# Score matmuls of two attention units in turns, with their PSUM banks shared with the weighted sums

## The chip, the cores and the metric

The kernel runs on one core of a Trainium2 chip. The metric is device time in microseconds (us) of one execution; lower is better. Engines are named as in the profile: PE (TensorE matmul), PEld (its weight loads), DVE (VectorE), ACT (ScalarE), POOL (GpSimd), SP (SyncE, which issues most DMAs). Matmul results go to PSUM, which has 8 banks of 128 partitions; a tile here takes one bank.

## The reference

Three stages follow each other: attention, a dense SoLU layer with layer norm, and a layer of eight experts of which each token uses one. Only the first is touched.

```python
def _attn_ref(q, k, v):                       # 4 batches, 8 heads, 576 positions, 64 columns
    scores = scale * np.matmul(q, k.transpose(0, 1, 3, 2))
    mask_local   = (rel >= 0) & (rel < 32)                       # heads 0 to 3
    mask_strided = (rel >= 0) & (pos[None, :] % 32 == pos[:, None] % 32)   # heads 4 to 7
    scores = np.where(masks, scores, -1e9)
    attn = exp(scores - max); attn = attn / (sum(attn) + 1e-9)
    return np.matmul(attn, v)
...
h = x @ w_in; solu = h * softmax(h); ln = layernorm(solu) * g_ln; x = ln @ w_out
e = argmax(x @ w_gate + bias[modality]); out = gate * (relu(x @ w1[e]) @ w2[e])
```

## The kernel before

**Attention.** Heads are handled in pairs `hp` (two heads, j = 0 and 1); pairs 0 and 1 are local, 2 and 3 strided. `qT` and `kT` hold a pair transposed: head 0 in partitions 0-63, head 1 in partitions 64-127 for local pairs. For strided pairs the sequence is cut into 8 residues (`SG = 8`, 72 positions each), and residue t stands in partitions 0-63 if it is even and in 64-127 if it is odd. A score matmul contracts over 64 rows, so it reads only one half of the partitions. Each pair gives four units of work. A local unit is three tiles of 96 queries by 128 keys of one head; a strided unit is four tiles of 72 by 72 of one head, all of even or all of odd residues. All tiles of one unit thus lie in one half of the partitions.

**One unit.** `scores` (line 311) issues its score matmuls (line 326) into one PSUM bank called S, DVE adds the mask and takes the maximum (line 332), POOL or DVE subtracts it (338), ACT takes the exponential (341), DVE sums (356) and takes reciprocals (357, 358), POOL normalises (364). `probs_T` transposes the result on PE (372, tile pP) and ACT copies it to pT (374). When both units of a head pair's group are there, `weighted` (377) multiplies with V into one bank called po (383); head j's sums go to output partitions 64j to 64j+63. ACT copies po to xTH (395) and DVE writes the remainder to xTL (396). Score and weighted-sum matmuls are float32, and the trace has two records for each of them.

**The dense layer** runs beside attention on the same engines: ph (line 475, x @ w_in), pn (518, transposes), pa and pb (531, @ w_out). The start also converts float64 weights: DVE, ACT and POOL work of lines 203 to 261 (wf, winH, winL, woH, woL).

**Banks.** Eight banks: "h" 2 (ph, and S of the first batch), "T" 2 (transposes), "y" 2 (pa, pb), "S" 1 (S of batches 1 to 3), "o" 1 (po).

**Order.** The kernel emits work in slots (a unit's stages A, T, P, V, and the table `TAKES` that says how many slots stand between dense steps). A scheduler then simulates a timeline and sets each engine's final order, and with it, tile by tile, which bank of a tag a tile gets. Engines run that order in sequence, so an instruction that waits holds up all behind it on its engine.

Of the kernel before, what the change touches and what calls it, by code (L numbers as in the profile page):

```python
# [9 lines left out]
F32 = mybir.dt.float32  # L10
# [18 lines left out]
def tile_attention_moe_moe2(  # L29
# [15 lines left out]
    nc = tc.nc  # L45
    B, H, S, D = q.shape
    NT, DM = out.shape
    NE, _, FF = w1.shape
    P = 128
    STRIDE = 32  # L50
# [75 lines left out]
    def flip_tile(out_, in_, eye):  # L126
        return nc.tensor.transpose(out_, in_, eye)

    warm_out = ps.tile([P, 2 * P], F32, name="warm", tag="S", bufs=1)

    def warm(n):
        wide = ident.bitcast(mybir.dt.bfloat16)
# [175 lines left out]
            dv = dst.rearrange("c (i p) -> c i p", p=SP_)[:, n * u:n * u + n]  # L308
        nc.scalar.copy(dv, pt[:, 0:n, :np_])

    def scores(b, hp, tiles, j, qT, kT):
        local = hp < H // 4
        nt = len(tiles)
        nq, nk = (QT, P) if local else (SP_, SP_)
        if b == 0:
            sp_ = ps.tile([P, 4, P], F32, name="S", tag="h")
        else:
            sp_ = ps.tile([P, 4, P], F32, name="S", tag="S", bufs=1)
        for i, t in enumerate(tiles):
            if local:  # L320
                half, q0, k0 = j, t * QT, t * QT
            else:
                half, q0 = t % 2, (j * SG + t) // 2 * SP_
                k0 = STRIDE + q0
            rows = slice(half * D, half * D + D)
            nc.tensor.matmul(  # L326
                sp_[:nq, i, :nk], qT[rows, q0:q0 + nq], kT[rows, k0:k0 + nk], start=True, stop=True)
        ex = at.tile([P, 4, P], F32, name="ex", bufs=4)
        mx = st.tile([P, 4], F32, name="mx")
        for i, t in enumerate(tiles):  # L330
            mk = maskL[:nq, min(t, 1)] if local else maskS
            nc.vector.tensor_tensor_reduce(  # L332
                ex[:nq, i, :nk], sp_[:nq, i, :nk], mk, 1.0, NEG, ALU.add, ALU.max,
                mx[:nq, i:i + 1])
        xb = SHIFT_ON[2 * b + (not local)]
        if xb != "0":
            eng = nc.gpsimd if xb == "P" else nc.vector
            eng.tensor_tensor(  # L338
                ex[:nq, :nt, :nk], ex[:nq, :nt, :nk],
                mx[:nq, :nt].unsqueeze(2).to_broadcast([nq, nt, nk]), ALU.subtract)  # L340
            nc.scalar.activation(ex[:nq, :nt, :nk], ex[:nq, :nt, :nk], AF.Exp, scale=SCALE)
            return ex, nq, nk, None
        nb = st.tile([P, 4], F32, name="nb")
        nc.vector.tensor_scalar(nb[:nq, :nt], mx[:nq, :nt], -SCALE, None, ALU.mult)
        den = st.tile([P, 4], F32, name="den")
        for i in range(nt):
            nc.scalar.activation(
                ex[:nq, i, :nk], ex[:nq, i, :nk], AF.Exp,
                bias=nb[:nq, i:i + 1], scale=SCALE, accum_out=den[:nq, i:i + 1])
        return ex, nq, nk, den  # L350
# [17 lines left out]
    def probs_T(tiles, ex, nq, nk):  # L368
        nt = len(tiles)
        pt = ps.tile([P, 4, P], F32, name="pP", tag="T")  # L370
        for i in range(nt):
            flip_tile(pt[:nk, i, :nq], ex[:nq, i, :nk], ident[:nq, :nq])
        pT = at.tile([P, 4, P], F32, name="pT", bufs=3)
        nc.scalar.copy(pT[:nk, :nt, :nq], pt[:nk, :nt, :nq])  # L374
        return pT

    def weighted(b, hp, tiles, nq, nk, pTs, vn):
        local = hp < H // 4
        nt, t0 = len(tiles), tiles[0]
        po = ps.tile([P, 4, P], F32, name="po", tag="o", bufs=1)  # L380
        for i, t in enumerate(tiles):
            for j in range(2):
                nc.tensor.matmul(  # L383
                    po[j * D:(j + 1) * D, i, :nq], vn[:nk, j, t], pTs[j][:nk, i, :nq],
                    start=True, stop=True)
        base = (b % 2) * S
        src = po[:, :nt, :nq]
        if local:
            o0 = base + t0 * QT
            dH, dL = [x[:, hp, o0:o0 + nt * QT].rearrange("c (t q) -> c t q", t=nt) for x in (xTH, xTL)]  # L390
        else:
            dH, dL = [
                x[:, hp, base:base + S].rearrange("c (p i) -> c i p", i=SG)[:, t0::2]
                for x in (xTH, xTL)]
        nc.scalar.copy(dH, src)
        nc.vector.tensor_tensor(dL, src, dH.bitcast(F32), ALU.subtract)

    def attention_slots():
        order = [(b, hp) for b in range(B) for hp in PAIRS[b]]
        units = []  # L400
        for b, hp in order:
            for tiles in ((0, 1, 2), (3, 4, 5)) if hp < H // 4 else ((0, 2, 4, 6), (1, 3, 5, 7)):
                for j in range(2):
                    units.append((b, hp, tiles, j))
        nat, tr, live = {}, {}, {}

        def load(n):
            if n < len(order):
                nat[n] = load_pair(*order[n])

        def transpose(n, part):
            if n < len(order):
                if part == 0:
                    tr[n] = alloc_pair(order[n][1])
                transpose_part(order[n][1], part, *nat[n][0:2], *tr[n])

        load(0)
        load(1)
        for part in range(4):
            transpose(0, part)  # L420
            warm(WARM)
        pts = {}

        def stage_a(n):
            if n < len(units):
                b, hp, tiles, j = units[n]
                live[n] = scores(b, hp, tiles, j, *tr[n // 4])
                normalise(b, hp, len(tiles), *live[n])

        def stage_t(n):  # L430
            if n < len(units):
                m, part = divmod(n, 4)
                transpose(m + 1, part)
                if part == 3:
                    load(m + 2)

        def stage_p(n):
            z = n - LAG
            if 0 <= z < len(units):
                b, hp, tiles, j = units[z]  # L440
                ex, nq, nk, den = live.pop(z)
                pts[z] = (probs_T(tiles, ex, nq, nk), nq, nk)

        def stage_v(n):
            z = n - LAG
            if 0 <= z < len(units):
                b, hp, tiles, j = units[z]
                if j == 1:
                    first, nq, nk = pts.pop(z - 1)
                    weighted(b, hp, tiles, nq, nk, (first, pts.pop(z)[0]), nat[z // 4][2])  # L450

        stages = dict(A=stage_a, T=stage_t, P=stage_p, V=stage_v)
        for n in range(len(units) + LAG):
            for c in STAGES:
                stages[c](n)
                yield

    def moe_a(t, front, between):
        g0 = (t % (NTILE // 2)) * P
        ts_ = slice(g0, g0 + P)  # L460
        e = mp.tile([P, 2, 512], F32, name="e")
        so = mp.tile([P, 2, 512], F32, name="so")
        mx = st.tile([P, 2], F32, name="hmx")
        hs = []
        for hf in range(2):
            if done_att and t % 2:
                ph = ps.tile([P, 512], F32, name="ph", tag=("S", "o")[hf], bufs=1)
            else:
                ph = ps.tile([P, 512], F32, name="ph", tag="h")
            hs.append(ph)  # L470
            cs = slice(hf * 512, hf * 512 + 512)
            n = 0
            for c in range(KD):
                for a, w in ((xTH, winH), (xTH, winL), (xTL, winH)):
                    nc.tensor.matmul(ph, a[:, c, ts_], w[:, c, cs], start=n == 0, stop=n == 3 * KD - 1)  # L475
                    n += 1
                if c == 1:
                    between()
            nc.vector.reduce_max(mx[:, hf:hf + 1], ph, axis=AX.X)
            if hf == 0:  # L480
                front()
                between(1)
        nb = st.tile([P, 1], F32, name="hnb")
        nc.vector.tensor_scalar(nb, mx[:, 0:1], mx[:, 1:2], -1.0, ALU.max, ALU.mult)
        s2 = st.tile([P, 2], F32, name="s2")
        for hf in range(2):
            nc.scalar.activation(e[:, hf], hs[hf], AF.Exp, bias=nb, scale=1.0, accum_out=s2[:, hf:hf + 1])
        a2 = st.tile([P, 2], F32, name="a2")
        for hf in range(2):
            nc.vector.scalar_tensor_tensor(  # L490
                so[:, hf], e[:, hf], 1.0, hs[hf], ALU.mult, ALU.mult, accum_out=a2[:, hf:hf + 1])
        return so, e, s2, a2
# [407 lines left out]
    def chunk_few(w, idx, j, side=(), then=None, blk=0, tiny=False):  # L900
# [6 lines left out]
        steps = TINY_STEPS if tiny else FEW_STEPS  # L907

        def up(q):
            p = ps.tile([P, 256], F32, name="pq", tag=("h", "h", "S", "o")[q], bufs=(2, 2, 1, 1)[q])  # L910
            f_ = slice(q * 256, q * 256 + 256)
            for c in range(KD):
                fl = dict(stop=c == KD - 1, skip_group_check=True)
# [299 lines left out]
```

## Time and profile before

| | |
|---|---|
| median of 3 runs (lowest to highest) | 718.24 us (717.89 to 719.5) |
| span of the profiled execution | 714.5 us, first to last instruction |
| median less span | 3.7 us |
| PE busy | 652.2 us, 91% of the span |
| DVE busy | 381.2 us, 53% |
| ACT busy, POOL busy | 298.5 us, 204.1 us |

The profiled execution has no time of its own beside its span; the 3.7 us by which the median of the runs is above the span is what lies around it. Attention's score matmuls run from 6.7 to 339.6 us of the span, its weighted sums from 18.5 to 355.8 us. Busy shares are means over stages with different limits, so the rows below are taken from stretches. PE intervals overlap, since matmuls are pipelined: what a matmul costs is read from one start to the next, not from its own duration.

### The profile page before, as it was taken

Reading aid. Unit: us, or ns where it says so; the run is one execution under the profiler, and the core shown is the slowest. Engines: PE = TensorE matmul, PEld = TensorE weight load, DVE = VectorE, ACT = ScalarE, POOL = GpSimd, SP = SyncE. Lnnn points to the kernel's source line nnn. Section 1 sums busy time; section 2 is a strip of 40 time slices with the busy share of each in tenths; the row PEclk is TensorE's granted clock in tenths of the full one; section 3 lists DMA queues with packets and bytes.
Section 4 is the critical chain, followed back from the end, with each engine's and each line's share of the span. In section 5 each row is a group of like instructions: output and inputs, shape, how many; then the busy total and the mean of one; then the engine's idle time right before and its main releaser. Section 6 shows DMA issues by size and latency. Waiting matters only on the chain. (4 is left out here: it accounts for less than half of the span.)

```text
span 714.5 us, 12636 instructions
## 1 busy us (share of the span) xinstructions
PE 652.2 (91%) x4540; PEld 565.4 (79%) x4540; DVE 381.2 (53%) x1361; ACT 298.5 (42%) x689; POOL 204.1 (29%) x253
## 2 busy tenths in 40 slices
PE   7688999999999999999999999999999999992954
PEld 6466877888888888888888998998898888882843
DVE  4999897567766666556488642235111121112761
ACT  3545654445545556667356421224111211211631
POOL 5876553111433242212003322232022112202410
PEclk9999978999999999999999999999999999996987
DMA  8735411023221122100061201446011011101770
GB/s 221 184 129 159 111 71 34 18 66 85 71 59 41 49 54 70 33 19 16 30 212 55 90 31 47 145 170 210 27 60 60 16 45 60 57 19 41 235 240 7
DMA packets 54696, 59.77 MB, mean 84 GB/s; under 512 B 39296, under 2 KB 39296, under 8 KB 54594
## 3 DMA queue, kind: packets, MB, share of 16 engines
q1 hardware_dynamic: 47954, 43.04, 20.5%
q0 software_dynamic: 4048, 10.78, 4.7%
q10 hardware_dynamic: 2592, 4.72, 1.9%
q8 instruction: 48, 0.79, 0.5%
q14 instruction: 54, 0.44, 0.2%
HBM read 48.79 MB, written 10.26 MB: 83 GB/s over the span
## 5 line engine op out<-in xcount | busy, mean ns | idle before, releaser
L881 DVE SCALAR_TENSOR_TENSOR winL<-pf,winL 128x512 fp32r<-128x512 f32 x36 | 24.9, 692 | 136.2 <-ACT winL L880 136.1
L834 PE MATMUL py<-w2H,winL 128*128 128x512 f32 x288 | 92.5, 396 | 0.0
L874 PE MATMUL pf<-xTH,w1H 128*128 128x256 f32 x288 | 82.4, 287 | 0.0
L874 PE MATMUL pf<-xTL,w1H 128*128 128x256 f32 x288 | 81.6, 283 | 0.0
L874 PE MATMUL pf<-xTH,w1L 128*128 128x256 f32 x288 | 81.5, 283 | 0.0
L364 POOL TENSOR_TENSOR ex<-ex,rd 96x384 f32<-96x384 f32 (+1 forms) x56 | 48.2, 863 | 100.1 <-DVE rd L358 69.2
L326 PE MATMUL S<-kT,qT 64*72 64x72 f32 (+1 forms) x448 | 63.5, 289 | 4.7 <-DVE mx L332 3.2
L880 ACT ACTIVATE winL<-pf 128x512 fp32r<-128x512 f32 x36 | 21.6, 599 | 99.7 <-PE pf L874 99.7
L834 PEld LDWEIGHTS py<-w2H,winL 128*128 128x128 f32 x288 | 53.5, 188 | 10.9
L326 PEld LDWEIGHTS S<-kT,qT 64*72 64x72 f32 (+1 forms) x448 | 49.3, 176 | 15.8 <-DVE mx L332 4.1
L475 PE MATMUL ph<-winH,xTH 128*128 128x512 f32 x144 | 61.1, 424 | 0.6 <-DVE so L490 0.5
L338 POOL TENSOR_TENSOR ex<-ex,mx 72x288 f32<-72x288 f32 (+1 forms) x40 | 34.6, 864 | 89.3 <-DVE mx L332 59.2
L475 PE MATMUL ph<-winH,xTL 128*128 128x512 f32 x144 | 58.8, 414 | 0.0
L475 PE MATMUL ph<-winL,xTH 128*128 128x512 f32 x144 | 58.8, 408 | 0.0
L874 PEld LDWEIGHTS pf<-xTH,w1H 128*128 128x128 f32 x288 | 56.4, 196 | 0.3
L874 PEld LDWEIGHTS pf<-xTL,w1H 128*128 128x128 f32 x288 | 56.4, 196 | 0.3
L874 PEld LDWEIGHTS pf<-xTH,w1L 128*128 128x128 f32 x288 | 56.4, 196 | 0.0
L840 POOL DMA_INDIRECT out_dram<-yo,idx x14 | 14.0, 1001 | 134.0 <-ACT yo L839 125.5
L531 PE MATMUL pa<-woH,nL 128*128 128x264 f32 x144 | 42.7, 296 | 1.3 <-DVE nL L521 1.3
L383 PE MATMUL po<-pT,vn 72*64 72x72 f32 (+1 forms) x448 | 37.4, 266 | 7.0 <-ACT pT L374 6.4
L531 PE MATMUL pa<-woH,nH 128*128 128x264 f32 x144 | 43.0, 299 | 0.4 <-ACT nH L520 0.4
L531 PE MATMUL pb<-woH,nH 128*128 128x256 f32 x144 | 41.4, 287 | 0.0
(257 smaller groups left out, 1657.7 us busy)
## 6 DMA issues: line engine op xcount, KB each, us to landing
raw<-in_moe_w_dram SPq DMA_DIRECT2D x37, 512.0 KB
y_d<-yt ACTq DMA_DIRECT2D x18, 256.0 KB
raw<-in_moe_w_in_dram SPq DMA_DIRECT2D x8, 512.0 KB
raw<-in_moe_w_out_dram SPq DMA_DIRECT2D x8, 512.0 KB
vn<-in_v_dram SPq DMA_DIRECT2D x16, 160.0 KB
qn<-in_q_dram SPq DMA_DIRECT2D x8, 288.0 KB
kn<-in_k_dram SPq DMA_DIRECT2D x8, 288.0 KB
vn<-in_v_dram SPq DMA_DIRECT2D x8, 288.0 KB
```

Source lines behind the costliest of these rows:

```text
L326: nc.tensor.matmul(sp_[:nq, i, :nk], qT[rows, q0:q0 + nq], kT[rows, k0:k0 + nk], start=True, stop=True)
L338: eng.tensor_tensor(ex[:nq, :nt, :nk], ex[:nq, :nt, :nk], mx[:nq, :nt].unsqueeze(2).to_broadcast([nq, nt, nk]), ALU.subtract)
L364: nc.gpsimd.tensor_tensor(ex[:nq, :nt, :nk], ex[:nq, :nt, :nk], rd[:nq, :nt].unsqueeze(2).to_broadcast([nq, nt, nk]), ALU.mult)
L383: nc.tensor.matmul(po[j * D:(j + 1) * D, i, :nq], vn[:nk, j, t], pTs[j][:nk, i, :nq], start=True, stop=True)
L475: nc.tensor.matmul(ph, a[:, c, ts_], w[:, c, cs], start=n == 0, stop=n == 3 * KD - 1)
L531: nc.tensor.matmul(p, a[:, f], w[:, f, cols], start=n == 0, stop=n == 3 * KF - 1)
L834: nc.tensor.matmul(p, a[:, f, s], x, start=n == 0, stop=n == 3 * KF - 1)
L840: nc.gpsimd.indirect_dma_start(out=out[:, :], out_offset=indirect(idx[:, col, 2:3].bitcast(U32)), in_=o, in_offset=None, bounds_check=NT - ...
L874: mm = nc.tensor.matmul(p[:, u], a[:, c, fs], x[:, c], start=n == 0, stop=n == 3 * KD - 1)
L880: last[0] = (nc.scalar.activation(hH[:, f2s], p, AF.Relu), nc.vector.scalar_tensor_tensor(hL[:, f2s], p, 0.0, hH[:, f2s].bitcast(F32), ALU ...
L881: nc.vector.scalar_tensor_tensor(hL[:, f2s], p, 0.0, hH[:, f2s].bitcast(F32), ALU.max, ALU.subtract))
```

## The change

The two units of a group become a pair that is laid out together. `raw_scores` is new: it takes two S banks at once, one for each half of the partitions, and issues the score matmuls of the two units in turns, first unit, second unit, first unit and so on. `scores` now only does what follows. Strided units are regrouped, so that unit u of group g holds the even (u = 0) or odd (u = 1) residues of both heads: tiles 4g+u and 4g+2+u for j = 0 and 1, and a group's four residues are contiguous. Before, a group held all even or all odd residues, and its two units were the two heads. The tag "S" has now two banks, which S and po share; "o" is gone. The dense layer's and the experts' uses of "S" and "o" become "S" throughout. Every engine has the same instructions as before, in the same number.

```diff
-    def scores(b, hp, tiles, j, qT, kT):
+    def raw_scores(b, hp, pair, qT, kT):
+        local = hp < H // 4
+        nq, nk = (QT, P) if local else (SP_, SP_)
+        banks = []
+        for _ in range(2):
+            if b == 0:
+                banks.append(ps.tile([P, 4, P], F32, name="S", tag="h"))
+            else:
+                banks.append(ps.tile([P, 4, P], F32, name="S", tag="S"))
+        for i in range(len(pair[0])):
+            for half in range(2):
+                t, j = pair[half][i]
+                if local:
+                    q0, k0 = t * QT, t * QT
+                else:
+                    q0 = (j * SG + t) // 2 * SP_
+                    k0 = STRIDE + q0
+                rows = slice(half * D, half * D + D)
+                nc.tensor.matmul(
+                    banks[half][:nq, i, :nk], qT[rows, q0:q0 + nq], kT[rows, k0:k0 + nk],
+                    start=True, stop=True)
+        return banks
...
-            sp_ = ps.tile([P, 4, P], F32, name="S", tag="S", bufs=1)
...
-        po = ps.tile([P, 4, P], F32, name="po", tag="o", bufs=1)
+        po = ps.tile([P, 4, P], F32, name="po", tag="S")
         for i, t in enumerate(tiles):
             for j in range(2):
+                half, at_ = place[t, j]
                 nc.tensor.matmul(
-                    po[j * D:(j + 1) * D, i, :nq], vn[:nk, j, t], pTs[j][:nk, i, :nq],
+                    po[j * D:(j + 1) * D, i, :nq], vn[:nk, j, t], pTs[half][:nk, at_, :nq],
                     start=True, stop=True)
...
-            for tiles in ((0, 1, 2), (3, 4, 5)) if hp < H // 4 else ((0, 2, 4, 6), (1, 3, 5, 7)):
-                for j in range(2):
-                    units.append((b, hp, tiles, j))
+            for g in range(2):
+                if hp < H // 4:
+                    pair = [[(t, j) for t in range(3 * g, 3 * g + 3)] for j in range(2)]
+                else:
+                    pair = [[(t, j) for t in (4 * g + u, 4 * g + 2 + u) for j in range(2)] for u in range(2)]
+                units += [(b, hp, pair, 0), (b, hp, pair, 1)]
...
-                ph = ps.tile([P, 512], F32, name="ph", tag=("S", "o")[hf], bufs=1)
+                ph = ps.tile([P, 512], F32, name="ph", tag="S")
```

What the scheduler makes of it differs by batch. First the order on PE at the first units of batch 0, in the kernel before (a number tells one tile from another; x4 is four matmuls in a row):

```order
L326 MATMUL S_181<-kT_148,qT_147 72x72 x4
L127 MATMUL ptq_202<-ident_77,qn_141 128x72 x4
L326 MATMUL S_218<-kT_148,qT_147 72x72 x4
L127 MATMUL ptq_247<-ident_77,qn_141 128x72 x4
L326 MATMUL S_263<-kT_148,qT_147 72x72 x4
```

and the same place after the change:

```order
L329 MATMUL S_181<-kT_148,qT_147 72x72
L329 MATMUL S_182<-kT_148,qT_147 72x72
L127 MATMUL ptq_207<-ident_77,qn_141 128x72 x4
L329 MATMUL S_181<-kT_148,qT_147 72x72
L329 MATMUL S_182<-kT_148,qT_147 72x72
L329 MATMUL S_181<-kT_148,qT_147 72x72
L329 MATMUL S_182<-kT_148,qT_147 72x72
L329 MATMUL S_181<-kT_148,qT_147 72x72
L329 MATMUL S_182<-kT_148,qT_147 72x72
L127 MATMUL ptq_247<-ident_77,qn_141 128x72 x4
```

Here the matmuls of the two units do stand in turns. Then a group of batch 1, S_1700 and its partner, on PE before:

```order
L383 MATMUL po_1691<-pT_1575,vn_817 64x96
L326 MATMUL S_1700<-kT_1217,qT_1216 72x72 x4
L127 MATMUL pn_1677<-ident_77,so_1315 128x128 x4
L127 MATMUL pn_1684<-ident_77,so_1315 128x128 x4
L383 MATMUL po_1691<-pT_1641,vn_817 64x96
L383 MATMUL po_1691<-pT_1575,vn_817 64x96
L383 MATMUL po_1691<-pT_1641,vn_817 64x96
L383 MATMUL po_1691<-pT_1575,vn_817 64x96
L383 MATMUL po_1691<-pT_1641,vn_817 64x96
L326 MATMUL S_1735<-kT_1217,qT_1216 72x72 x4
```

and after, where S_1701 is the second unit of S_1700's pair:

```order
L396 MATMUL po_1691<-pT_1580,vn_817 64x96
L329 MATMUL S_1700<-kT_1221,qT_1220 72x72 x4
L127 MATMUL pn_1677<-ident_77,so_1315 128x128 x4
L127 MATMUL pn_1684<-ident_77,so_1315 128x128 x4
L396 MATMUL po_1691<-pT_1641,vn_817 64x96
L396 MATMUL po_1691<-pT_1580,vn_817 64x96
L396 MATMUL po_1691<-pT_1641,vn_817 64x96
L396 MATMUL po_1691<-pT_1580,vn_817 64x96
L396 MATMUL po_1691<-pT_1641,vn_817 64x96
L329 MATMUL S_1701<-kT_1221,qT_1220 72x72 x4
```

Nothing has moved here: the two units stand as far apart as two units did before, and in the built program S_1700 and S_1701 have the same bank, po_1691 the other. Last, a strided weighted sum of batch 3 on PE, before:

```order
L383 MATMUL po_4165<-pT_4096,vn_3591 64x72
L326 MATMUL S_4230<-kT_4007,qT_4006 72x72 x4
L475 MATMUL ph_4497<-winH_71,xTH_75 128x512
```

and after, from the score matmuls that had the same bank just before it:

```order
L329 MATMUL S_4064<-kT_3682,qT_3681 72x72 x4
L127 MATMUL pP_4158<-ident_77,ex_4025 72x72 x4
L396 MATMUL po_4165<-pT_4101,vn_3591 64x72 x2
L329 MATMUL S_4176<-kT_4012,qT_4011 72x72 x4
L127 MATMUL pP_4203<-ident_77,ex_4073 72x72 x4
```

Before, one po matmul stood alone and seven followed when the second unit's pT was there; now two stand together and six follow, and po_4165 takes the bank that S_4064 had.

## Rows read from the trace of the kernel before

**Rows 1.** The page: span, and busy time of each engine.

```profile
span 714.5 us, 12636 instructions
PE 652.2 (91%) x4540; PEld 565.4 (79%) x4540; DVE 381.2 (53%) x1361; ACT 298.5 (42%) x689; POOL 204.1 (29%) x253
```

**Rows 2.** Stretches: from:to, length, busy us of each engine, clock, DMA share, GB/s.

```profile
18.00:36.00 18.00, 11.26 (x86) 9.07 (x86) 17.96 (x60) 10.13 (x23) 15.36 (x19) 1.00 0.76 186
...
72.00:126.00 54.00, 51.46 (x313) 41.84 (x313) 46.15 (x156) 30.44 (x73) 23.16 (x28) 0.87 0.24 71
126.00:360.00 234.00, 233.33 (x1878) 199.26 (x1877) 145.27 (x729) 127.12 (x358) 56.04 (x82) 1.00 0.17 47
```

**Rows 3.** The longest wait of PE, 72 to 486 us: total, times, longest.

```profile
PE po L383 <- ACT pT L374: 1.5, 1, 1.5
```

**Rows 4.** Score and weighted-sum matmuls by line, behind 126 us: ns min/median/max.

```profile
L326 PE MATMUL S<-kT,qT x288: 225/225/348, 132.3 to 339.6; 64*72 64x72 f32 x96, 64*96 64x128 f32 x48
...
L383 PE MATMUL po<-pT,vn x312: 226/236/297, 135.9 to 355.8; 72*64 72x72 f32 x96, 128*64 128x96 f32 x60
```

**Rows 5.** Score matmuls in flight (x) in stretches of 0.12 us.

```profile
20.44:20.56 0.12, 0.12 (x4) 1.00 1.04 16
...
20.92:21.04 0.12, 0.12 (x7) 1.00 1.33 19
```

**Rows 6.** Timeline of PE: start us, busy us, line, operation, count.

```profile
156.31 0.34 PE L383 MATMUL po<-pT,vn 72*64 72x72 f32 x2
156.58 0.39 PE L531 MATMUL pb<-woH,nH 128*128 128x256 f32 x1
...
159.09 0.28 PE L531 MATMUL pb<-woH,nH 128*128 128x256 f32 x1
159.21 0.28 PE L531 MATMUL pb<-woL,nH 128*128 128x256 f32 x1
159.42 0.71 PE L383 MATMUL po<-pT,vn 72*64 72x72 f32 x14
160.06 0.39 PE L531 MATMUL pb<-woH,nL 128*128 128x256 f32 x1
160.28 0.41 PE L127 MATMUL pP<-ident,ex 72*72 72x72 f32 x4
160.63 0.73 PE L326 MATMUL S<-kT,qT 64*72 64x72 f32 x8
161.30 1.09 PE L127 MATMUL pn<-ident,so 128*128 128x128 f32 x8
```

**Rows 7.** Timeline, two S units: the PE instruction behind each, DVE's last read.

```profile
133.45 0.38 PE L554 MATMUL pb<-woH,onesR 128*128 128x256 f32 x1
134.17 0.08 DVE L332 DVE_READ_ACCUMULATOR2_ANT mx<- 72x1 f32 x1
...
163.96 0.47 PE L127 MATMUL ptq<-ident,qn 96*128 96x96 f32 x3
165.05 0.08 DVE L332 DVE_READ_ACCUMULATOR2_ANT mx<- 72x1 f32 x1
```

**Rows 8.** Timeline near 104 us (brackets: idle before, releaser), and two stretches.

```profile
103.93 0.71 PE L383 MATMUL po<-pT,vn 128*64 128x96 f32 x10 [1.47 <-ACT pT L374]
104.57 0.47 PE L127 MATMUL pP<-ident,ex 96*128 96x96 f32 x3
108.27 0.45 DVE L396 TENSOR_TENSOR xTL<-po,xTH 128x288 fp32r<-128x288 f32 x1
...
102.00:108.00 6.00, 4.53 (x32) 3.69 (x32) 6.00 (x24) 5.17 (x16) 1.51 (x1) 0.77 0.00 0
108.00:114.00 6.00, 6.00 (x23) 4.75 (x23) 3.89 (x15) 2.01 (x4) 1.36 (x2) 0.66 0.23 52
```

**Rows 9.** Timeline of the start: first weight piece on ACT, then on DVE.

```profile
12.11 0.67 ACT L209 ACTIVATE mag<-raw 128x512 f32<-128x512 f32 x1 [2.05 <-DMA raw<-in_moe_w_in_dram]
...
13.92 1.54 DVE L214 SCALAR_TENSOR_TENSOR wf<-mag,raw 128x512 int32<-128x512 int32 x1
```

More of the change, by code (lines that the diff above doesn't have):

```diff
@@ L127, in flip_tile @@
         return nc.tensor.transpose(out_, in_, eye)
-    warm_out = ps.tile([P, 2 * P], F32, name="warm", tag="S", bufs=1)
+    warm_out = ps.tile([P, 2 * P], F32, name="warm", tag="S")
     def warm(n):
@@ L309, in transpose_part, with scores @@
         nc.scalar.copy(dv, pt[:, 0:n, :np_])
-    def scores(b, hp, tiles, j, qT, kT):
+    def raw_scores(b, hp, pair, qT, kT):
[20 more added lines that the diff above has]
+        return banks
+    def scores(b, hp, tiles, sp_):
         local = hp < H // 4
@@ L314, in scores @@
         nq, nk = (QT, P) if local else (SP_, SP_)
-        if b == 0:
-            sp_ = ps.tile([P, 4, P], F32, name="S", tag="h")
-        else:
-            sp_ = ps.tile([P, 4, P], F32, name="S", tag="S", bufs=1)
[L319 to L327, printed above, removed]
         ex = at.tile([P, 4, P], F32, name="ex", bufs=4)
         mx = st.tile([P, 4], F32, name="mx")
-        for i, t in enumerate(tiles):
+        for i, (t, j) in enumerate(tiles):
             mk = maskL[:nq, min(t, 1)] if local else maskS
@@ L375, in probs_T, with weighted @@
         return pT
-    def weighted(b, hp, tiles, nq, nk, pTs, vn):
+    def weighted(b, hp, pair, nq, nk, pTs, vn):
         local = hp < H // 4
+        place = {tj: (half, i) for half in range(2) for i, tj in enumerate(pair[half])}
+        tiles = sorted({t for t, _ in place})
         nt, t0 = len(tiles), tiles[0]
-        po = ps.tile([P, 4, P], F32, name="po", tag="o", bufs=1)
+        po = ps.tile([P, 4, P], F32, name="po", tag="S")
         for i, t in enumerate(tiles):
             for j in range(2):
+                half, at_ = place[t, j]
                 nc.tensor.matmul(
-                    po[j * D:(j + 1) * D, i, :nq], vn[:nk, j, t], pTs[j][:nk, i, :nq],
+                    po[j * D:(j + 1) * D, i, :nq], vn[:nk, j, t], pTs[half][:nk, at_, :nq],
                     start=True, stop=True)
@@ L392, in weighted @@
             dH, dL = [
-                x[:, hp, base:base + S].rearrange("c (p i) -> c i p", i=SG)[:, t0::2]
+                x[:, hp, base:base + S].rearrange("c (p i) -> c i p", i=SG)[:, t0:t0 + nt]
                 for x in (xTH, xTL)]
@@ L422, in attention_slots @@
         pts = {}
+        banks = [None, None]
         def stage_a(n):
             if n < len(units):
-                b, hp, tiles, j = units[n]
-                live[n] = scores(b, hp, tiles, j, *tr[n // 4])
-                normalise(b, hp, len(tiles), *live[n])
+                b, hp, pair, half = units[n]
+                if half == 0:
+                    banks[:] = raw_scores(b, hp, pair, *tr[n // 4])
+                live[n] = scores(b, hp, pair[half], banks[half])
+                normalise(b, hp, len(pair[half]), *live[n])
         def stage_t(n):
@@ L439, in stage_p @@
             if 0 <= z < len(units):
-                b, hp, tiles, j = units[z]
+                b, hp, pair, half = units[z]
                 ex, nq, nk, den = live.pop(z)
-                pts[z] = (probs_T(tiles, ex, nq, nk), nq, nk)
+                pts[z] = (probs_T(pair[half], ex, nq, nk), nq, nk)
         def stage_v(n):
@@ L446, in stage_v @@
             if 0 <= z < len(units):
-                b, hp, tiles, j = units[z]
-                if j == 1:
+                b, hp, pair, half = units[z]
+                if half == 1:
                     first, nq, nk = pts.pop(z - 1)
-                    weighted(b, hp, tiles, nq, nk, (first, pts.pop(z)[0]), nat[z // 4][2])
+                    weighted(b, hp, pair, nq, nk, (first, pts.pop(z)[0]), nat[z // 4][2])
         stages = dict(A=stage_a, T=stage_t, P=stage_p, V=stage_v)
@@ L909, in up @@
         def up(q):
-            p = ps.tile([P, 256], F32, name="pq", tag=("h", "h", "S", "o")[q], bufs=(2, 2, 1, 1)[q])
+            p = ps.tile([P, 256], F32, name="pq", tag=("h", "h", "S", "S")[q])
             f_ = slice(q * 256, q * 256 + 256)
```

## The prediction, made before the changed kernel had run

> **What bounds the kernel now.** I read the page first: PE is busy 91% of the span, the next engine 53% [rows 1]. A mean hides stages, so I cut the span into stretches [rows 2]. In the first of them, 18 to 36 us, DVE is busy 17.96 of 18 us while PE has 11.26: DVE bounds the start (weight conversion and softmax together), and PE time saved there buys nothing. From 72 to 126 us both are nearly full (PE 51.46 of 54, DVE 46.15). From 126 to 360 us PE is busy 233.33 of 234 us and DVE 145.27: PE alone bounds. The waits say the same: from 72 to 486 us the longest wait of PE in total is 1.5 us, once [rows 3]. So a microsecond of PE time saved behind 126 us is a microsecond of the end, as long as no new wait eats it. 288 score records lie there, two for each of 144 matmuls [rows 4].
>
> Score matmuls of different halves do overlap on this chip, and the kernel before shows it once. At 20 us, where two units from different halves happen to stand side by side, 4 are in flight with one unit and 7 with both [rows 5]. That speed is what the change could bring. Whether it does is decided by the order.
>
> **The change, part by part.**
>
> *Turns.* In batch 0 the order shows turns (S_181, S_182, S_181, ...); of its eight pairs five stand so close that their halves can overlap. All of them lie in the start that DVE bounds. Value: 0. The cover is DVE's queue; without it each of the five would save at least what a strided unit takes behind 126 us, 0.67 us from 160.63 to 161.30 [rows 6], 3.4 us in all. In batches 1 to 3 there are no turns: in the order after, at least seven matmuls stand between the two units of every one of the 24 pairs, and in the built program 23 of the 24 have both units in one bank, with po mostly in the other. The second unit has to wait until DVE has read the first, as before, and the scheduler fills that wait with other work, as before (the S_1700 piece is the same in both orders). Overlap gained behind 126 us: none, 0 us.
>
> The overlap at 20 us [rows 5] was between units in two banks of the built program. The Trainium skill, "TensorEngine Tiling (Array Packing)", Restrictions and Gotchas, says that different row tiles can't use the same PSUM bank at the same time. No row here shows such a case. By that rule the first rival below is out altogether, whatever the order; the sum stays at 0 for this part.
>
> *Weighted sums.* The two heads' matmuls go to different output partitions and run as twos: 14 records from 159.42 to the next start at 160.06 are 0.64 us, while one matmul alone (2 records) takes 156.31 to 156.58, 0.27 us [rows 6]. Seven matmuls are three twos and a single one, four steps; one alone is a step. So a step is (0.64 - 0.27) / 3 = 0.12 us, whether it holds one matmul or two. A strided group had 1 + 7 matmuls, five steps; now it has 2 + 6, four steps. Behind 126 us there are 12 strided groups (96 matmuls of that shape, eight to a group [rows 4]): 12 x 0.12 = 1.5 us saved. Local groups stay at 1 + 5. This part needs no overlap of score matmuls.
>
> *Switches.* PE pays when it goes to or from the score and weighted-sum matmuls: pb starts 0.12 us after pb (159.09, 159.21), but po 0.21 us after pb (159.42) [rows 6]. That is 0.09 us a switch; I take the same for the way back. Counted in the two orders from the first ph to the last po, the switches fall from 204 to 194, since po and S stand next to each other more often: 10 x 0.09 = 0.9 us saved. It could be nothing, if some of the ten lie before 126 us or switches between S and po cost more than the 0.09: 0 to 0.9, taken 0.9.
>
> *Shared banks.* A tile now can wait for a tile of the other kind. From the next PE start behind a unit to DVE's last read the fast case takes 134.17 + 0.08 - 133.45 = 0.80 us, one with DVE work between 165.05 + 0.08 - 163.96 = 1.17 us [rows 7]. Two places in the order after stand closer than that. S_4064 and po_4165 share a bank with only four pP between, which take 160.28 to 160.63, 0.35 us [rows 6]: a wait of 0.45 to 0.82. S_2713 and S_2714 have four ptq and three pP between, about 0.6 us by the same row: 0.2 to 0.57. All else on PE queues behind them, so both count in full: 0.65 to 1.4, taken 0.9 us lost (nearer to the fast case, since DVE has room there).
>
> *The start.* A strided unit now reads both heads, so it needs all four transposed parts where it needed two, and the first pair stands behind the next pair's first transposes: its units end later or earlier by up to a microsecond. DVE's full load begins with the first weight piece at 13.92 us, and that waits for a DMA and ACT at 12.11 us [rows 9], not for attention; DVE is still idle in between before. DVE, ACT and PE have the same list of instructions ahead of the first dense tile in both orders. Effect 0, bounds -1 to +1 us.
>
> *The rest* (dH and dL slices, ph and the experts' tiles in "S" instead of "S" and "o") has the same instructions and bank count: 0.
>
> Sum: -1.5 - 0.9 + 0.9 = -1.5 us against the profiled span of 714.5, so 713.0. The median of the runs stands 3.7 us above that span, and nothing of the change lies outside it: 718.24 - 1.5 = 716.8 us. Bounds of the parts: best -1.5 - 0.9 + 0.65 - 1 = -2.8 (715.5), worst -1.5 + 1.4 + 1 = +0.9 (719.1).
>
> **The rivals.**
>
> 1. *It does what it says.* The halves overlap behind 126 us after all. A strided pair would take little over the 0.67 us of one unit instead of 1.34. For about 20 pairs (144 score matmuls there) that is 20 x 0.67 = 13 us: 705 us. For it: the seven in flight at 20 us. Against it: the order and the banks.
>
> 2. *The savings drown.* Gains of 2.4 us are spread over 230 us, and each is a tenth of a microsecond; if each of the bank places that stand at 1.3 to 1.7 us apart (six or so) also costs 0.2 us, and the switches give nothing, it is 718.2, no change. For it: the order before was free of waits, and this one has other neighbours.
>
> 3. *Slower: the shared bank behind DVE's queue.* Place: the first score unit of batch 1, S_841, which takes the bank of po_756; before, the two had different banks. Where DVE is full, a po bank is held long: the po matmuls at 103.93 end before 104.57, and DVE's remainder ends at 108.27 + 0.45, 4.15 us later [rows 8]. Between po_756's last matmul and S_841 stand 13 matmuls (14 records), 54 / 313 = 0.17 us each in that stretch [rows 2], 2.4 us. So PE would stand 1.8 us. And the clock: behind the idle 1.47 us at 103.93 the granted clock was 0.77 and 0.66 in the next two stretches of 6 us [rows 8], so part of each ran at 1.2 instead of 2.4 GHz: 0.23 x 6 + 0.34 x 6 = 3.4 us of full-speed time. Together 716.8 + 1.8 + 3.4 = 722.0. It decides from the point where po_756 is read later than 2.4 us after its last matmul. Against it: DVE has a little room between 72 and 84 us, and the scheduler put S_841 behind it knowing the bank.
>
> 4. *The clock gives back.* The same two stretches at a lower clock are in the kernel before; with other neighbours one of them may vanish: -3.4 us, 713.4. Nothing in the rows speaks for or against it.
>
> **How the numbers follow.** About 0.2% (1.4 us) is what a measurement of this kernel can tell from no change, so the forecast lies at that edge. Forecast 0.50 (0.28 of it faster, 0.22 same), rival 1 0.04, rival 2 0.16 (0.02 faster by luck, 0.14 same), rival 3 0.18 (slower), rival 4 0.12 (faster). Faster 0.28 + 0.04 + 0.02 + 0.12 = 0.46, same 0.36, slower 0.18. The likeliest case has 715.5 to 719.1. The range of 8 in 10 leaves out rival 1, the lower half of rival 4 and a little over half of rival 3: 713.3 to 721.0.
>
> **What would show it.** After: score units behind 126 us still start alone, with 0.67 us from a strided unit's start to the next start; po runs of 4 and 12 records in place of 2 and 14, at about 0.28 and 0.53 us; waits of PE on DVE's last read (mx, line 342) of half a microsecond near 240 and 325 us; DVE full up to 72 us as before, first ph within a microsecond of where it was. Wrong it is if score records come in turns behind 126 us, if PE shows waits of more than 2 us on xTL or mx there, or if a stretch at the lower clock appears or goes.

## The result: 0.8% slower, where 0.2% faster was forecast

| | before | after |
|---|---|---|
| median (lowest to highest), 20 runs each | 719.1 us (716.61 to 723.35) | 724.95 us (723.04 to 728.75) |
| span of the profiled execution | 714.5 us | 723.0 us |

The ratio is 1.0083, 95% interval 1.0065 to 1.0101. The forecast was 716.8 us, with 713.3 to 721.0 as its range.

The page after, span and busy time, answers to [rows 1]. PE has 2 us less work than before in a span that is 8.5 us longer:

```profile
span 723.0 us, 12634 instructions
PE 650.1 (90%) x4540; PEld 563.5 (78%) x4540; DVE 378.2 (52%) x1361; ACT 297.8 (41%) x689; POOL 200.4 (28%) x253
```

The stretches of [rows 2] after the change. Columns: from:to, length, busy us of PE, PEld, DVE, ACT and POOL (instructions), granted clock, DMA share, GB/s:

```profile
18.00:36.00 18.00, 10.07 (x78) 7.83 (x77) 17.28 (x51) 7.07 (x15) 14.26 (x16) 1.00 0.58 140
72.00:126.00 54.00, 52.91 (x319) 42.19 (x317) 43.17 (x156) 31.87 (x76) 24.33 (x29) 0.83 0.24 71
126.00:360.00 234.00, 232.62 (x1886) 199.35 (x1887) 148.75 (x738) 127.63 (x358) 57.37 (x85) 1.00 0.17 48
```

Next to nothing is lost between 126 and 360 us; PE is as full there as before. The waits of PE from 72 to 486 us, which answer to [rows 3], show where something new stands:

```profile
PE px L127 <- DVE nL L540: 4.5, 1, 4.5
...
PE po L396 <- DVE mx L342: 0.3, 1, 0.3
```

One wait of 4.5 us, on work that the change does not touch; the next longest is 0.9 us. Following the same events through both traces gives the account of the 8.5 us by which the spans differ. The last column is how much later an event is after the change.

| event | before | after | later by |
|---|---|---|---|
| first ph | 67.8 us | 71.9 us | 4.1 |
| first pa | 130.1 | 134.2 | 4.1 |
| pa, record 400 of 448, counted from 0 | 408.0 | 408.0 | 0.0 |
| first px (transposes of the early gather) | 408.8 | 413.2 | 4.4 |
| first pf (experts' first layer) | 415.4 | 422.0 | 6.7 |
| end of the span | 714.5 | 723.0 | 8.5 |

So the start loses 4.1 us, the stretch that PE bounds gives all of it back, and then 4.4 us are lost by the wait and 2.3 more behind it. These 2.3 us are the clock, as the rows below show. The last 1.8 us up to the end of the span come later: 1.3 of them stand near 500 us, where PE waits 3.8 us in all for gathered tokens (xg) instead of 2.8; no run was made on that. PE after the change, around the wait (start, busy us, line, operation, form, count, and in brackets the idle time before with its releaser):

```profile
408.46 0.28 PE L550 MATMUL pb<-woL,nH 128*128 128x256 f32 x1
413.24 1.12 PE L127 MATMUL px<-ident,xgE 128*128 128x128 f32 x4 [4.50 <-DVE nL L540]
...
415.25 0.42 PE L550 MATMUL pa<-woL,nH 128*128 128x264 f32 x1
415.47 0.42 PE L550 MATMUL pa<-woH,nL 128*128 128x264 f32 x1
...
419.05 0.28 PE L550 MATMUL pa<-woL,nH 128*128 128x264 f32 x1
419.17 0.28 PE L550 MATMUL pa<-woH,nL 128*128 128x264 f32 x1
```

Behind the wait the same matmul takes 0.22 us from start to start, at 419 us 0.12 us: PE ran at 1.2 instead of 2.4 GHz until 418 us (granted clock 0.50 from 413.2 to 418 us). In the kernel before the clock stays full there (1.00).

px needs a bank that nL (a remainder, pn less nH, made on DVE) must first have read. What nL waits for stands on DVE:

```profile
406.49 0.21 DVE L523 TENSOR_SCALAR rstd<-rstd,var 128x1 f32<-128x1 f32 x1 [0.30 <-ACT e L517]
...
407.16 0.18 DVE L598 TENSOR_REDUCE rg<-rex 128x4 f32<-128x32 f32 x1
411.57 0.16 DVE L526 TENSOR_TENSOR sc<-rstd,rs 128x1 f32<-128x1 f32 x1 [4.24 <-POOL rstd L524]
...
412.52 0.66 DVE L540 TENSOR_TENSOR nL<-pn,nH 128x512 fp32r<-128x512 f32 x1
```

DVE's part of rstd (one over the standard deviation) is there at 406.7 us, but the rest of it (a power, on POOL) comes back only at 411.5 us. On POOL it stands behind the four early gathers (xgE, line 824), and these wait for a table that six chained scatters (tab_d, line 624) must have filled. A scatter or gather here is a DMA that POOL issues by a list of row numbers:

```profile
386.41 1.18 POOL L624 DMA_INDIRECT tab_d<-entry,rpos  x1 [6.64 <-DVE LG L557]
...
401.36 1.03 POOL L624 DMA_INDIRECT tab_d<-entry,rpos  x1 [1.61 <-DMA y_d<-yt]
406.19 0.98 POOL L824 DMA_INDIRECT xgE<-y_d,idxE  x1 [3.80 <-issue]
...
409.99 0.95 POOL L824 DMA_INDIRECT xgE<-y_d,idxE  x1 [0.30 <-issue]
410.95 0.59 POOL L524 TENSOR_TENSOR rstd<-rstd,mhalf 128x1 f32<-128x1 f32 x1
```

The order on POOL was the same in the kernel before, only earlier:

```profile
384.19 1.06 POOL L605 DMA_INDIRECT tab_d<-entry,rpos  x1 [5.10 <-DVE rpos L603]
...
401.10 1.02 POOL L805 DMA_INDIRECT xgE<-y_d,idxE  x1 [3.20 <-DMA y_d<-yt]
...
406.25 0.59 POOL L505 TENSOR_TENSOR rstd<-rstd,mhalf 128x1 f32<-128x1 f32 x1 [0.33 <-DVE rdif L565]
```

There rstd ended at 406.84 us, the moment at which DVE asked for it (sc), and nL let the bank go at 408.77, the moment at which PE came for it (px). DVE and PE before:

```profile
406.88 0.16 DVE L507 TENSOR_TENSOR sc<-rstd,rs 128x1 f32<-128x1 f32 x1
...
408.11 0.66 DVE L521 TENSOR_TENSOR nL<-pn,nH 128x512 fp32r<-128x512 f32 x1
```

```profile
408.51 0.28 PE L531 MATMUL pb<-woL,nH 128*128 128x256 f32 x1
408.83 0.66 PE L127 MATMUL px<-ident,xgE 128*128 128x128 f32 x4
```

After the change the first scatter is 2.2 us later, since DVE computes its positions later (rpos at 385.97 instead of 383.75 us). From it to the first gather 19.8 us pass instead of 16.9; the scatters follow each other after 2.4 to 3.7 us instead of 2.4 to 2.5, and no run was made on the reason. PE arrives at the same time as before.

### The profile page after: what moved, and what is told of

Same layout as the page of the kernel before. It is cut to its first block, busy times and chain, and to the rows that moved or that the text cites. A ratio compares the mean times of both kernels' runs of the same rounds, so it can differ in the third digit from the quotient of the medians.

```text
span 723.0 us, 12634 instructions
## 1 busy us (share of the span) xinstructions
PE 650.1 (90%) x4540; PEld 563.5 (78%) x4540; DVE 378.2 (52%) x1361; ACT 297.8 (41%) x689; POOL 200.4 (28%) x253
## 5 line engine op out<-in xcount | busy, mean ns | idle before, releaser
L329 PE MATMUL S<-kT,qT 64*72 64x72 f32 (+1 forms) x448 | 59.0, 288 | 14.6 <-DVE mx L342 14.3
L374 POOL TENSOR_TENSOR ex<-ex,rd 96x384 f32<-96x384 f32 (+1 forms) x56 | 46.7, 837 | 84.2 <-DVE rd L368 52.5
L329 PEld LDWEIGHTS S<-kT,qT 64*72 64x72 f32 (+1 forms) x448 | 45.3, 175 | 26.1 <-DVE mx L342 13.3
L550 PE MATMUL pb<-woL,nH 128*128 128x256 f32 x144 | 41.5, 288 | 0.0
L550 PE MATMUL pa<-woL,nH 128*128 128x264 f32 x144 | 41.5, 288 | 0.0
```

The costliest lines, as they stand in the source:

```text
L329: nc.tensor.matmul(banks[half][:nq, i, :nk], qT[rows, q0:q0 + nq], kT[rows, k0:k0 + nk], start=True, stop=True)
L374: nc.gpsimd.tensor_tensor(ex[:nq, :nt, :nk], ex[:nq, :nt, :nk], rd[:nq, :nt].unsqueeze(2).to_broadcast([nq, nt, nk]), ALU.mult)
L550: nc.tensor.matmul(p, a[:, f], w[:, f, cols], start=n == 0, stop=n == 3 * KF - 1)
```

## The experiments

Two places were open at first: the start, where the change is made, and the wait at 408 us, a late effect of moved work. The first expectations number three theories: 1, the turns hold the start back; 2, any rebuilt order falls where it likes, by work that the edit does not name; 3, the shared banks cost. Theory G, of the gathers, came when the first four runs were known.

### One part of the change at a time

Turns undone (e1), each unit issuing its own matmuls:

```diff
+        for i, (t, j) in enumerate(tiles):
...
-        for i in range(len(pair[0])):
-            for half in range(2):
-                t, j = pair[half][i]
...
```

> The changed kernel with the turns undone: each unit again takes its bank and issues its own score matmuls; regrouping and shared banks stay. Theory 1 (turns hold the start back, the tail then loses more): the first ph is back from 71.9 to about 68 us, PE's wait on mx ahead of it (2.8 us) is gone, and the time falls from 725 by the start's 4 us to about 721; if the early gather also comes in time, to 716 to 718. Theory 2 (any rebuilt order falls where it likes, the turns do nothing): first ph anywhere, time 722 to 727. Theory 3 (the shared banks cost): first ph near 72, time about 725.

Measured: 730.45 us, ratio to before 1.0149 (1.0104 to 1.0194). That is slower than any of the three theories had it. The first ph is at 73.3 us, so the turns did not hold the start back: without them it is no earlier. The wait on nL is there again, 4.2 us.

Regrouping alone (e2; the edit of e1, with S and po in banks of their own):

```diff
-        po = ps.tile([P, 4, P], F32, name="po", tag="S")
+        po = ps.tile([P, 4, P], F32, name="po", tag="o", bufs=1)
```

> The kernel before with only the strided units regrouped; no turns, S and po in banks of their own. Theory 1: start as before (first ph within 1 us of 67.8), the weighted sums behind 126 us save about 1.5 us, time 717 to 719 against 719 before. Theory 2 (any rebuilt order falls where it likes): the time is off by 2 us or more either way, by a wait at the early gather near 408 us. Theory 3: same as before, 719.

Measured: 733.69 us, 1.0211 (1.015 to 1.0273), first ph at 73.4 us. Theory 2 alone had a loss of this kind. PE stands for 5.5 us at 405 us, on another instruction (pa, behind LG on DVE), but the trace shows the same chain on DVE (sc, 8.55 us idle ahead of it, released by rstd on POOL):

```profile
406.98 0.16 DVE L518 TENSOR_TENSOR sc<-rstd,rs 128x1 f32<-128x1 f32 x1 [8.55 <-POOL rstd L516]
```

Shared banks alone (e3):

```diff
-            sp_ = ps.tile([P, 4, P], F32, name="S", tag="S", bufs=1)
+            sp_ = ps.tile([P, 4, P], F32, name="S", tag="S")
...
-        po = ps.tile([P, 4, P], F32, name="po", tag="o", bufs=1)
+        po = ps.tile([P, 4, P], F32, name="po", tag="S")
```

> The kernel before with only the banks shared: S and po take turns in two banks, units and their order of emission as before. Theory 1: start as before, a little saved behind 126 us, time 718 to 719. Theory 2: off by 2 us or more either way, by a wait at the early gather. Theory 3 (shared banks cost): PE waits on xTL or mx of more than 2 us in all, time 721 to 724.

Measured: 721.25 us, 1.003 (0.9995 to 1.0064): no difference that can be told, perhaps a little slower. From the first pa to record 400 PE needs 274.7 instead of 277.9 us, and px has no wait. So theories 1 and 3 fall: undoing the turns does not help, and the shared banks alone do not cost. The regrouping is in each kernel so far that is slower, but its start (5.6 us late in e1 and e2) is not all of its loss.

### The wait at 408 us

The transposes px one dense step later in the changed kernel (e4):

```diff
-        if t == NTILE - 1:
+        if t == NTILE:
             transpose_x(xgE[0])
```

> The changed kernel with the transposes of the first early gather (px) emitted one dense step later, behind 48 matmuls (about 6 us) more. Theory 1: the 4.7 us wait at 408 us and the lower clock behind it (together 6.6 us) are gone; what is left is the start's 4 us less the 4 us saved behind 126 us, and the later gather: 718 to 720. Theory 2 (the wait is not on the path, something else late in the tail holds the end): 724 to 726.

Measured: 724.89 us, 1.0069 (1.004 to 1.0098), as slow as the changed kernel. A miss, and a useful one: px has moved, the wait has not. It is now the next instruction in the queue that stands:

```profile
PE pa L550 <- DVE nL L540: 5.0, 2, 4.5
```

So the gathered data were not what PE waited for; nL was. That led to theory G: nL waits for rstd, and rstd stands on POOL behind the gathers. The edit for it (e5) queues the gathers behind the last rstd on POOL (`powers[-1]`) and keeps px one step later:

```diff
-                gather(xgE[j], idxE, j, 1 + EARLY_T * P)
...
+        if t == NTILE:
+            for j in range(EARLY):
+                gather(xgE[j], idxE, j, 1 + EARLY_T * P, behind=powers[-1])
```

> The changed kernel with one edit on POOL: the four early gathers stand behind the last rstd of the dense layer instead of ahead of it (and their transposes px one dense step later, so that they have time). The run with px alone moved kept a 4.7 us wait at 410 us, now of pa on nL. Theory G (PE waits for nL, nL waits on DVE behind sc, sc waits for rstd, and rstd stands on POOL behind gathers that wait for their table): the wait of 4.7 us is under 1 us, the lower clock behind it (3.4 us of full-speed time) is gone as well, 717 to 720 us. Rival (the gathers' data themselves are late): the wait moves to px, 723 to 726.

Measured: 718.76 us, 0.999 (0.9964 to 1.0016). The changed kernel's whole loss is gone with one step of POOL's order (e4, which has px moved alone, kept it). POOL, and the same place on PE:

```profile
399.77 1.03 POOL L624 DMA_INDIRECT tab_d<-entry,rpos  x1 [1.64 <-DMA tab_d<-entry,rpos]
405.25 0.60 POOL L524 TENSOR_TENSOR rstd<-rstd,mhalf 128x1 f32<-128x1 f32 x1 [4.45 <-DVE rdif L584]
406.27 1.02 POOL L825 DMA_INDIRECT xgE<-y_d,idxE  x1 [0.42 <-ACT yt L556]
```

```profile
406.96 0.28 PE L550 MATMUL pb<-woL,nH 128*128 128x256 f32 x1
407.54 0.39 PE L550 MATMUL pa<-woH,nL 128*128 128x264 f32 x1 [0.30 <-DVE nL L540]
```

The clock from 360 to 440 us is 1.00 in this run, 0.96 in the changed kernel. The same edit in the kernel before (e6):

> The kernel before with the same edit of POOL's order as a control. In it the chain rstd to nL ends with 0.5 us of PE waiting, so theory G expects little: 717.5 to 719.5 us, and a second profile of a start that is the same as before's. If the start of this profile is more than 1.5 us off before's (first ph at 67.8 us), part of the 4.1 us seen in the changed kernel's start is a difference between executions and not between kernels.

Measured: 718.57 us, 0.9996 (0.9971 to 1.0021); first ph at 68.4 us. There was nothing to gain, and nothing to spare either, as the opposite test shows. In the kernel before, POOL gets eight spare operations between the last gather (`late[-1]`) and rstd (e9):

```diff
+            for _ in range(8):
+                busy = nc.gpsimd.tensor_tensor(spare, ones[:, 0:1], mhalf, ALU.pow)
+                queue_after(busy, late[-1])
...
+        if t == NTILE:
+            queue_after(powers[-1], busy)
```

> The kernel before with eight spare operations on POOL (0.57 us each, 4.6 us in all, results not used) between the four early gathers and the last rstd of the dense layer; PE's order is unchanged. Theory G (in the kernel before this chain ends just in time, with no slack): PE's wait behind the first pa and pb of the last step goes from nothing to 4 to 5 us, the granted clock falls behind it, and the time rises by 4 to 8 us, to 723 to 727. Rival (the chain has slack in the kernel before, and the changed kernel's loss has another source): 719 to 720.

Measured: 726.37 us, 1.0095 (1.0058 to 1.0132). POOL and PE:

```profile
407.55 5.00 POOL L1018 TENSOR_TENSOR spare<-ones,mhalf 128x1 f32<-128x1 f32 x8
412.52 0.55 POOL L505 TENSOR_TENSOR rstd<-rstd,mhalf 128x1 f32<-128x1 f32 x1
```

```profile
410.06 0.28 PE L531 MATMUL pb<-woL,nH 128*128 128x256 f32 x1
414.52 1.12 PE L127 MATMUL px<-ident,xgE 128*128 128x128 f32 x4 [4.18 <-DVE nL L521]
```

Five microseconds on an engine that is busy 29% of the span make the kernel before as slow as the changed one, by the same wait and (first pf 2.2 us later again than px) the same clock. Theory G is shown from both sides; why the gathers came later in the changed kernel is another question, which no run settles.

### What the start is worth

Batch 0 as in the kernel before, all else as changed (e7):

```diff
+                elif b == 0:
+                    pair = [[(t, j) for t in range(g, SG, 2)] for j in range(2)]
...
+                if b == 0:
+                    banks[half] = raw_scores(b, hp, pair, (half,), *tr[n // 4])[half]
```

> The changed kernel with batch 0 as in the kernel before: strided groups of one parity, no turns; batches 1 to 3 and the banks as changed. Theory S (the start is late because a strided unit reads both heads, and so needs all four transposed parts; turns give a little of that back): first ph back from 71.9 to within 1 us of what the kernel before shows, PE's waits on mx before 126 us down from 14.3 us to about 3, time about 721 with the wait at 408 us still there, 717 without it. Rival (the start's 4 us are the shared banks or a difference between executions): first ph 70 to 72, time 723 to 726.

Measured: 724.68 us, 1.0057 (1.003 to 1.0085). The start is back: first ph at 68.1 us, and PE's waits on mx before 126 us, here in the changed kernel and then in this one:

```profile
PE S L329 <- DVE mx L342: 14.3, 5, 3.9
```

```profile
PE S L325 <- DVE mx L338: 2.8, 2, 1.9
```

But the time is the changed kernel's; theory S had about 721. Executions differ in the start too. With batch 0 as before the first ph stands at 67.8 to 70.2 us in seven profiles (e12, with po in other banks, has 72.3), with batch 0 as changed at 71.9 to 72.9 us in four. So the loss is there, but 4.1 us is its size in one pair of profiles. At the first pa 1.4 us of the 3.8 are left, at 408 us 0.8, and then the wait on nL takes 4.7 us where it took 4.5: PE arrives earlier at a chain that is 0.5 us earlier itself (rstd at 410.44 us). With both repairs (e10):

> The changed kernel with both repairs: batch 0 as before, and the early gathers behind the last rstd. If the start's loss and the chain's loss add up, 718.8 (gathers alone) less the 0.8 to 2 us by which the run with batch 0 as before was ahead near 126 to 400 us: 716.5 to 718. Rival (what is gained in the start is waited for again later, at the next transfer): 718.5 to 719.5.

Measured: 721.36 us, 1.0018 (0.999 to 1.0045), against 0.999 for the gathers alone; both cases of the expectation had less. No gain from the start can be told. Shared banks alone with the gathers behind rstd (e11):

> The kernel before with shared banks and the gathers behind the last rstd, no regrouping and no turns. The stretch from 130 to 408 us was 3.2 us shorter with shared banks alone; its profile had a start 2.5 us late in which the order on PE is the same as before's, so that much is a difference between executions. Expected 716 to 718; if the shared banks cost something in the start, 718.5 to 721.

Measured: 719.75 us, 0.9992 (0.9963 to 1.0021): no difference either, where 716 to 718 was expected.

### Turns that are made

Turns enforced in batches 1 to 3 of the changed kernel (e8):

```diff
+                mm = nc.tensor.matmul(
+                    banks[half][:nq, i, :nk], qT[rows, q0:q0 + nq], kT[rows, k0:k0 + nk], ...)
+                if prev and b > 0:
+                    queue_after(mm, prev)
```

> The changed kernel with turns really made in batches 1 to 3: each score matmul of a pair is queued behind the one before it in the written order, so that the two units stand in two banks and all but the first matmul of a pair follow in turns. The rival of the prediction 'it does what it says': a strided pair takes 0.75 to 0.85 us for its eight matmuls instead of 1.34, 24 pairs save 10 to 13 us of PE time, and the stretch 126 to 360 us is that much shorter less what PE waits for a second bank; 714 to 718 us with the wait at the early gather still there. Against: if matmuls of different halves do not overlap in turns, 0.17 us from start to start, nothing saved, and new waits on po or mx: 726 to 732.

Measured: 725.13 us, 1.0082 (1.0047 to 1.0117), between the two cases of the expectation. The turns work. Fourteen records, seven matmuls of two units, take 0.66 us to the next start:

```profile
156.72 0.73 PE L336 MATMUL S<-kT,qT 64*72 64x72 f32 x14
157.38 0.32 PE L127 MATMUL pP<-ident,ex 72*72 72x72 f32 x2
```

In [rows 6] a unit's four took 0.67 us. From the first pa to record 400 the score matmuls take 22.8 us (each start to the next, waits left out) instead of 30.4. What became of the 7.6 us stands in the waits of PE and the stretch from 126 to 360 us:

```profile
PE pP L127 <- POOL ex L384: 5.7, 3, 2.0
PE S L336 <- DVE xTL L419: 2.1, 2, 1.4
```

```profile
126.00:360.00 234.00, 222.86 (x1823) 189.48 (x1824) 140.04 (x720) 125.15 (x354) 57.81 (x87) 0.95 0.17 47
```

PE is idle for 11.1 us there, and its clock is 0.95 where it was 1.00. More than half of the idle time are transposes pP that wait for the normalising on POOL; that the units now come in bursts is a reading of it, not measured. A second form gave each unit of a pair its own bank and put po among the transposes' banks, with both repairs (e12):

```diff
-                banks.append(ps.tile([P, 4, P], F32, name="S", tag="S"))
+        banks = {u: ps.tile([P, 4, P], F32, name="S", tag=f"S{u}", bufs=1) if b else ...
...
-        po = ps.tile([P, 4, P], F32, name="po", tag="S")
+        po = ps.tile([P, 4, P], F32, name="po", tag="T")
```

> Both repairs, and turns made real in batches 1 to 3 in a way that blocks less: the two units of a pair have a bank each of their own (S0, S1), and po takes its bank from the transposes' two. In the run with forced turns and shared banks the score matmuls took 22.8 instead of 30.4 us, and PE's idle time from 130 to 408 us rose from 1.4 to 12.3 us. If the idle time came from the sharing of two banks by three tiles, it falls to 3 or 4 us here and the time is 711 to 715. Rival (the idle time comes from units that come in bursts, so that pP waits for POOL's normalising, or from po among the transposes): idle 8 us or more, 717 to 724.

Measured: 725.81 us, 1.0084 (1.005 to 1.0118). The score matmuls take 19.3 us, 11 us less than before, and PE's idle time is still 12.8 us from the first pa to record 400, now in many small waits (the largest sum from 126 to 360 us is 2.2 us, ph on xTH). So the sharing of two banks by S and po was not the reason; po among the transposes can be one, and no run tells it from the rest. No version here is faster than the kernel before.

## Why the prediction was wrong, point by point

**Turns: 0 us.** Right. Score matmuls behind 126 us still take 30.4 us from start to start, before and after. The step that stood behind it, that the order makes no turns in batches 1 to 3, held; what turns could bring was put at 13 us in rival 1, and the runs that made them (e8, e12) show 7.6 and 11 us of PE time, all of it lost to new waits and a lower clock. So rival 1 was not out "whatever the order": once the turns were forced, the two units stood in two banks. No run has two halves in one bank at the same time.

**Weighted sums: -1.5 us.** Right: -1.4 us (20.57 to 19.21 us in all, each start to the next, waits left out). The runs of four and of twelve records take 160.49 - 160.21 = 0.28 and 163.84 - 163.32 = 0.52 us, where 0.28 and 0.53 were forecast:

```profile
160.21 0.35 PE L396 MATMUL po<-pT,vn 72*64 72x72 f32 x4
160.49 0.34 PE L329 MATMUL S<-kT,qT 64*72 64x72 f32 x2
...
163.32 0.60 PE L396 MATMUL po<-pT,vn 72*64 72x72 f32 x12
163.84 0.38 PE L550 MATMUL pb<-woL,nH 128*128 128x256 f32 x1
```

**Switches: -0.9 us, and shared banks: +0.9 us.** Mis-sized, to the good. The other kinds of matmul (ph, pn, pa, pb, pP, ptq, pr) took 224.7 us before and 222.5 after, 2.2 us less; how much of that is switches was not tried alone. Of the two waits on a shared bank one of 0.3 us is there. Together the stretch from the first pa to record 400 fell from 277.9 to 273.8 us (277.3 and 276.8 in e6 and e9, which have the order before). Shared banks alone have 274.7 and 275.7 (e3, e11), so the part that was put at a loss of 0.9 us goes with some of the gain.

**The start: 0, bounds -1 to +1 us.** Wrong in place, and nearly right in effect by luck. The first ph is 4.1 us later. That goes with the regrouping (e2, e7); by the program, a regrouped unit needs all four transposed parts, and a pair in turns both banks. PE stands 14.3 us on mx, ph with it. That DVE's load waits "not for attention" did not hold: DVE waits for its score units too (10.7 us before 126 us, where it was 6.7). But undoing it gained nothing that can be told.

**The step that failed** is the one ahead of the sum: "So a microsecond of PE time saved behind 126 us is a microsecond of the end, as long as no new wait eats it." The list of PE's waits in [rows 3] was read as slack, and the sum has no term for the chain on POOL and DVE behind 360 us. The list shows what waited, not how near others were. The chain rpos, scatters, gathers, rstd, sc, nL ended exactly when PE came in the kernel before, so it is as critical as PE though it shows no wait there. After the change it ended 4.7 us later (rstd at 410.95 instead of 406.25 us), while PE came at the same time. That is +6.8 us (4.5 and the clock's 2.3), the whole loss by e5 (724.95 to 718.76, 6.2 us). The late start alone did not make the chain late: with the first ph back at 68.1 us (e7) rstd still stood at 410.44 us.

**The rivals.** Slower was given 0.18, with S_841 behind po_756's bank as its place. PE has no wait over 0.2 us from 72 to 126 us after the change, so that mechanism did not come. Its form did, elsewhere: a few microseconds of wait and some more from the clock. A stretch at the lower clock that appears was also among the prediction's signs of being wrong.

What moved the chain was not tried by itself and stays open. For the 2.2 us ahead of the first scatter the trace has a candidate: DVE has six weight conversions (xTH and xTL from raw, 3.8 us) between rhi and rpos after the change, where it had two (1.3 us):

```profile
379.78 0.15 DVE L618 TENSOR_SCALAR rhi<-rlo 128x6 int32<-128x6 int32 x1
...
381.66 2.48 DVE L771 TENSOR_TENSOR xTL<-raw,w2H 128x512 fp32r<-128x512 f32 x4
...
385.97 0.15 DVE L622 SCALAR_TENSOR_TENSOR rpos<-rlo,rhi 128x6 int32<-128x6 int32 x1
```

## What to carry to other kernels

No wait in a list of waits does not mean slack: before a saving on the bounding engine is counted, follow the other chains that meet it later (here index tables, gathers and one small operation queued behind them) and read by how much each was early. An operation that another engine waits for should not stand in a queue behind one that waits for a DMA, however idle that engine is on average. A matmul made faster only counts if what feeds it and what empties it keep pace.

## What the runs showed of the hardware that was not expected

Matmuls over 64 rows from the two halves of the partitions, in turns and into two banks, take 0.66 / 7 = 0.09 us each (e8); from one half alone 0.67 / 4 = 0.17 us [rows 6].

How long PE runs at 1.2 GHz behind the first ph differs between executions of one order. This counts the stretches that the trace records at half the clock, and what lies between the first ph and the first record of the clock. From the first ph to the first pa it is 13.0 us in e6's profile, 17.0 in before's and 22.9 in e9's, which have the same order on PE up to there, and 19.0 in e7's and 29.6 in e10's, which share another. e10 takes 69.7 us for that stretch and e7 64.7: 5.0 more, as (29.6 - 19.0) / 2 = 5.3 would have it. But the kernel before and e6 both take 62.3 or 62.4 us, with PE idle 1.4 us longer in e6, so the clock alone does not set the length. In e10 the step comes at 88.6 us, seen in ph's starts, 0.43 us apart ahead of it and 0.23 behind:

```profile
87.16 0.63 PE L495 MATMUL ph<-winL,xTH 128*128 128x512 f32 x1
87.59 1.06 PE L495 MATMUL ph<-winH,xTL 128*128 128x512 f32 x2
...
88.76 0.39 PE L495 MATMUL ph<-winL,xTH 128*128 128x512 f32 x1
88.99 0.38 PE L127 MATMUL pt<-ident,wf 128*128 128x128 f32 x2
```

The clock's column does not show it. It reads 1.00 here, since the trace has no record of the clock ahead of 88.6 us in this run:

```profile
84.00:90.00 6.00, 6.00 (x23) 4.52 (x22) 1.88 (x6) 1.20 (x3) 1.45 (x2) 1.00 0.00 0
```

So a single profile does not tell the start's price to a microsecond, and the spans of two profiles (8.5 us apart) can differ by more than the medians of the kernels (5.9 us).
